# Attention in turns of a whole pair of heads, with the clusters placed by ScalarE

## The chip, the cores and the metric

The kernel runs on one core of a Trainium2 chip. The metric is the device time of one execution in microseconds; for each kernel several executions are timed and their median is given. A profile of one execution shows what every engine did. The engines are TensorE (PE in the profile; its weight loads are PEld), VectorE (DVE), ScalarE (ACT), GpSimd (POOL) and SyncE (SP, which only issues transfers). Each has a queue of its own and they meet by semaphores.

## The reference

Two stages. The first is attention in which a query sees only the keys of its own cluster; the second sends each token to one of eight experts.

```python
B, H, S, D, C = 4, 8, 768, 64, 16
q_assign = argmax(q_n @ c_n.T)               # nearest of 16 centroids, all normalised
k_assign = argmax(k_n @ c_n.T)
mask   = q_assign[..., :, None] == k_assign[..., None, :]
scores = where(mask, scale * q @ k.T, -1e9)
attn   = softmax(scores);   attn_out = attn @ v
x = attn_out as rows (3072 tokens, 512)
expert_idx = argmax(x @ w_gate);  gate_w = softmax(x @ w_gate)[expert_idx]
y[rows of e] = relu(x[rows of e] @ w1[e]) @ w2[e]      # 8 experts, 512 -> 1024 -> 512
out = gate_w[:, None] * y
```

Inputs are random and in float32.

## The kernel before

The attention works on pairs of heads, `g` from 0 to 15 (4 batches, 4 pairs each); one head of a pair lies on partitions 0 to 63, the other on 64 to 127. A pair has 12 scores (two halves of the queries, six tiles of 128 keys). The mask is part of the score: the clusters of queries and keys, written as one-hots into `ohT` (the keys' scaled so that other clusters get a huge negative number), are multiplied and added to q times k in the same bank of PSUM. The engines' instructions stand in the order in which the program names them (a manual schedule), and each engine keeps to its order.

```python
def score(u):                                  # one of 12 of a pair
    ps = ps_s.tile([P, 2, 512], F32, name="sps")          # one of 3 buffers of two banks
    for a in range(2): matmul(ps[:, a, 0:HS], lhsT=qk[g][r, 1, ks],  rhs=qk[g][r, 0, qs], start=True,  stop=False)
    for a in range(2): matmul(ps[:, a, 0:HS], lhsT=ohT[g][r, 1, ks], rhs=ohT[g][r, 0, qs], start=False, stop=True)
    A[u] = ap.tile([P, 2, HS], F32, name="A")
    nc.scalar.activation(A[u], ps[:, :, 0:HS], AF.Exp, scale=D**-0.5)
    if j == 1: T = A[u-1] + 1e-9/P + A[u]                 # VectorE
    elif j > 1: T = T + A[u]                              # VectorE

def attend(u):                                 # O (64 rows of each head) += v.T @ A[u]
    for a in range(2): matmul(O[g, half][a*D:(a+1)*D, 0:HS], lhsT=rows[g, "v"][:, a, j, :], rhs=A[u][:, a, :], ...)

def finish(g, half): nc.scalar.copy(XT[g][:, half...], O[g, half])
def turn_blocks(g):  # VectorE turns q and k of a pair, two instructions
def similar(g):      # 4 matmuls with the centroids into a score buffer; VectorE turns the result (sim)
def assign(g):       # VectorE: maximum, is_ge; GpSimd: times first_c
def assign2(g):      # VectorE: maximum, is_equal, and the turn of the one-hots (ohs)
def put_k(g):        # VectorE: scale (kv, two instructions), then four transfers kv -> ohT
def put_q(g):        # ScalarE: four copies ohs -> ohT
def weigh(g):        # 12 matmuls: row sums (T) and gate logits (XT) into the bank mps; VectorE turns it (ls)
def keep(g, c0, c1): # VectorE turns XT (xb); four stores from GpSimd to x_rows
...
# the routing of the first three batches, worked out while the last batch is attended:
choose, count, slots1, one_hots1(0), one_hots1(1), tokens1, spread1   # VectorE, TensorE, some GpSimd
gather1(0), gather1(1)                                                # GpSimd: indirect loads of x_rows
turn_rows1                                                            # VectorE: xu, the rows turned
first_half(0, ...)                                                    # first layer of expert 0
```

PSUM before: three score buffers of two banks (`ps_s`), one bank for the products (`ps_o`), one for everything small (`ps_m`, the tile `mps`). The loop takes turns of six (`NB = 6`), with jobs put between them by `at(turn, part, job)`:

```python
for n in range(-4, NTURN + 5):
    for x in range(n * NB, (n + 1) * NB):
        score(x)                      # (jobs of part 2 after the fifth)
    jobs of part 0                    # weigh, turn_blocks, similar, put_q, ...
    for x in range(n * NB, (n + 1) * NB):
        attend(x)
    jobs of part 1                    # finish, assign2, put_k, keep, ...
```

Of the kernel before, what the change touches and what calls it, by code (L numbers as in the profile page):

```python
# [20 lines left out]
NB = 6  # L21
# [164 lines left out]
def kernel(  # L186
# [14 lines left out]
    P = 128  # L201
# [65 lines left out]
    ps_o = late.enter_context(tc.tile_pool(name="ps_o", bufs=1, space=PSUM))  # L267
    ps_m = late.enter_context(tc.tile_pool(name="ps_m", bufs=1, space=PSUM))
# [12 lines left out]
    def blocks_of(g):  # L281
        return sum(g["n"]) // 32

# [355 lines left out]
    def count(part):  # L639
        ps = ps_m.tile([P, 512], F32, name="mps")  # L640
        last = part["pr"][:, :, part["n"] - 1]
        nc.tensor.matmul(ps[:, 0:E], lhsT=lt_strict, rhs=last, start=True, stop=True)
        nc.tensor.matmul(ps[:, E : 2 * E], lhsT=ones_sq, rhs=last, start=True, stop=True)
        nc.vector.tensor_copy(part["cnt"].rearrange("p a e -> p (a e)"), ps[:, 0 : 2 * E])
# [67 lines left out]
    def spread(pool, parts, w, gi):  # L712

        ps = ps_m.tile([P, 512], F32, name="mps")
        for i in range(4):
            nc.tensor.matmul(
                ps[:, i * 2 * w : (i + 1) * 2 * w],
                lhsT=k_["spread"][:, i, :], rhs=parts, start=True, stop=True,
            )
        v = ps[:, 0 : 8 * w].rearrange("p (i h w) -> p h w i", h=2, w=w)  # L720
        tv, ta = numbers(pool, v[:, 0], v[:, 1], [P, w, 4])
        nc.vector.tensor_scalar(tv, ta, scalar1=4.0, scalar2=k_["quarter"], op0=ALU.mult, op1=ALU.add)
        nc.vector.tensor_copy(gi, tv)
# [5 lines left out]

    msched = ExitStack()  # L730
    msched.enter_context(tc.manual_schedule())
    with ExitStack() as actx:
# [4 lines left out]
        ap = actx.enter_context(tc.tile_pool(name="ap", bufs=NB + 1))  # L737
# [3 lines left out]
        xtp = actx.enter_context(tc.tile_pool(name="xtp", bufs=2))  # L741
# [34 lines left out]
        def load_v(g):  # L776
            b, hp = divmod(g, HP)
            t = rows[g, "v"] = ld.tile([P, 2, NQ, D], F32, name="v_in", bufs=3)
            nc.sync.dma_start(
                out=t.rearrange("p a j d -> p a (j d)"),  # L780
                in_=v[b, 2 * hp : 2 * hp + 2].rearrange("a (p j) d -> p a (j d)", j=NQ),
            )
# [13 lines left out]
        def idle_of(n):  # L796
            idle(ps_m.tile([P, 512], F32, name="mps"), n)

        ps = ps_m.tile([P, 512], F32, name="mps")
# [57 lines left out]
        def blocks():  # L857
            cps = ps_m.tile([P, 512], F32, name="mps")
            nc.tensor.transpose(cps[:, 0:P], cn.rearrange("p a d -> p (a d)"), ident)
            cview = cps[:, 0:P].rearrange("p (g a c) -> p g a c", a=2, c=C)  # L860
            for a in range(2):
                nc.vector.tensor_copy(cblk[a * D : (a + 1) * D, :, a, :], cview[a * D : (a + 1) * D, :, a, :])
# [79 lines left out]
        def put_q(g):  # L942

            t = sims.pop(g)
            for half in range(2):
                for a in range(2):
                    i, r, cols = places(half, a)
                    nc.scalar.copy(ohT[g][r, 0, cols], t[i])

        def put_k(g):  # L950

            t, kv = sims[g], asg.tile([P, 2, HS], BF16, name="kv")
            ohT[g] = ohTs[g % 2]
            for a in range(2):
                nc.vector.tensor_scalar(
                    kv[D:P, a, :], t[D:P], scalar1=big[D:P, a, 0:1], scalar2=big[D:P, a, 1:2], op0=ALU.mult, op1=ALU.add
                )
            for half in range(2):
                for a in range(2):
                    i, r, cols = places(half + 2, a)  # L960
                    nc.sync.dma_start(out=ohT[g][r, 1, (half * HS) : (half + 1) * HS], in_=kv[i, a, :])
# [22 lines left out]
        def score(u):  # L984
# [12 lines left out]
            if j == 1:  # L997
                T[g, half] = tp_.tile([P, 2, HS], F32, name="T", bufs=3)
                nc.vector.scalar_tensor_tensor(  # L999
                    T[g, half], in0=A[u - 1], scalar=1e-9 / P, in1=A[u], op0=ALU.add, op1=ALU.add  # L1000
                )
            elif j > 1:
                nc.vector.tensor_tensor(T[g, half], T[g, half], A[u], op=ALU.add)  # L1003
# [18 lines left out]
        rds, pads = {}, {}  # L1022

        def weigh(g):
# [4 lines left out]
            ps = ps_m.tile([P, 512], F32, name="mps")  # L1029
# [26 lines left out]
        def keep(g, c0, c1):  # L1056

            b, hp = divmod(g, HP)
            xb = xtp.tile([P, S], F32, name="xb")
            nc.vector.transpose(xb[:, 0 : c1 - c0], XT[g][:, c0:c1])  # L1060
            for quad in range(4):
                nc.gpsimd.dma_start(  # L1062
                    out=x_d[b * S + c0 : b * S + c1, quad, hp * 32 : (hp + 1) * 32].rearrange("(n t) d -> t n d", t=32),
                    in_=xb[quad * 32 : (quad + 1) * 32, 0 : c1 - c0].rearrange("p (n d) -> p n d", d=32),
                )
# [44 lines left out]
        TG = UG // NB  # L1110
        TH = NQ // NB
        NTURN = NG * TG
        at(0, 1, place_consts)
        at(6, 1, place_consts2)
        for g in range(NG):
            n = g * TG
            if g == 0:
                at(-4, 0, turn, g, 0)
                at(-4, 0, load_next)
                at(-4, 0, blocks)  # L1120
                at(-4, 1, turn, g, 1)
                at(-3, 0, similar, g)
                at(-3, 0, assign, g)
                at(-3, 0, assign2, g)
                at(-3, 0, put, g)
            elif g == 1:
                at(-2, 1, idle_of, 20)
                at(0, 0, turn_blocks, g)
                for f in (similar, assign, assign2, put_k):
                    at(0, 1, f, g)  # L1130
                at(1, 0, put_q, g)
            else:
                at(n - 3, 0, turn_blocks, g)
                at(n - 2, 0, similar, g)
                at(n - 2, 0, assign, g)
                at(n - 2, 1, assign2, g)
                at(n - 2, 1, put_k, g)
                at(n - 1, 0, put_q, g)
            at(n, 1, finish, g, 0)
            at(n + 1, 1, finish, g, 1)  # L1140
            if g < NG - 1:
                at(n + 2, 0, weigh, g)
                at(n + 2, 1, keep, g, 0, S)
                if g % HP == HP - 1:
                    at(n + 3, 0, gate, g // HP)
                    at(n + 4, 0, gate2, g // HP)
# [18 lines left out]
        def tokens1():  # L1165
            ps = ps_m.tile([P, 512], F32, name="mps")[:, 0 : 2 * NP]
            tokens(ps, oh_r1, oh_c1, NF)
            rc1[1] = indices(pl, ps, NP, s_idx1)
# [21 lines left out]

        n = (NG - HP) * TG
        at(n + 1, 1, choose, pl, front)
        at(n + 2, 1, count, front)
        at(n + 2, 1, slots1)
        at(n + 3, 0, one_hots1, 0)
        at(n + 3, 1, one_hots1, 1)
        at(n + 5, 2, tokens1)
        at(n + 5, 1, spread1)
        at(n + 5, 1, gather1, 0)
        at(n + 6, 1, gather1, 1)  # L1200
        at(n + 7, 0, turn_rows1, 0)

        n = NG * TG
        at(n - 1, 0, keep, NG - 1, 0, HS)
        at(n, 0, weigh, NG - 1)
        at(n, 0, keep, NG - 1, HS, S)
        at(n, 0, first_half, 0, 0, FB // 4)
        at(n, 0, gate, B - 1)
        at(n, 0, gate2, B - 1)
        at(n, 0, keep_pads, B - 1)  # L1210
        at(n, 0, turn_rows1, 1)
        at(n, 1, first_half, 0, FB // 4, FB // 2)
        at(n + 1, 0, first_half, 0, FB // 2, FB)
        for g in range(2, NG):
            at(max(g * TG - 6, -1), 1, load_qk, g)
            at(max(g * TG - 5, -1), 1, load_v, g)
        for b in range(B - 1):

            at((b + 1) * HP * TG + 2, 1, keep_pads, b)
# [14 lines left out]
        for e in range(2):  # L1234
            for i in range(DB):
                at(HP * TG * (e + 1) - 4 + 2 * i + 1, 0, early, e, i)

        for n in range(-4, NTURN + 5):
            for x in range(n * NB, (n + 1) * NB):
                if 0 <= x < NU:  # L1240
                    score(x)
                if x == n * NB + 4:
                    for f, a in jobs.get((n, 2), ()):
                        f(*a)
            for f, a in jobs.get((n, 0), ()):
                f(*a)
# [3 lines left out]
            for f, a in jobs.get((n, 1), ()):  # L1250
                f(*a)


    mctx = ExitStack()
# [4 lines left out]
    with tc.tile_pool(name="sm", bufs=1) as sm:  # L1259
# [34 lines left out]
        tok_ps = ps_m.tile([P, 512], F32, name="mps")[:, 0 : 2 * NC]  # L1294
# [19 lines left out]
        bps = ps_m.tile([P, 512], F32, name="mps")[:, 0:1]  # L1314
# [178 lines left out]
```

## Time and profile before

| | |
|---|---|
| time, median of 3 runs | 712.38 us (711.19 to 713.41) |
| span of the profiled execution | 716.9 us |
| TensorE busy | 686.9 us (96%) |
| VectorE busy | 484.6 us (68%) |
| ScalarE busy | 266.9 us (37%) |
| GpSimd busy | 251.1 us (35%) |
| attention, first score to last product | from 15.2 to 342.1 us |

A line of a group reads: line of the kernel, engine, operation, written tile <- read tiles, shape, count | busy us, mean ns of one | idle time of the engine just before them and what ended most of it. A line of a timeline reads: start in us, length in us, engine, line, operation and tiles, how many were merged into it, and in brackets how long the engine was idle before it and who ended that. A float32 matmul is recorded as two.

### The profile page before, as it was taken

Reading aid. Unit: us, or ns where it says so; the run is one execution under the profiler, and the core shown is the slowest. Engines: PE = TensorE matmul, PEld = TensorE weight load, DVE = VectorE, ACT = ScalarE, POOL = GpSimd, SP = SyncE. Lnnn points to the kernel's source line nnn. Section 1 sums busy time; section 2 is a strip of 40 time slices with the busy share of each in tenths; the row PEclk is TensorE's granted clock in tenths of the full one; section 3 lists DMA queues with packets and bytes.
Section 4 is the critical chain, followed back from the end, with each engine's and each line's share of the span. In section 5 each row is a group of like instructions: output and inputs, shape, how many; then the busy total and the mean of one; then the engine's idle time right before and its main releaser. Section 6 shows DMA issues by size and latency. Waiting matters only on the chain.

```text
span 716.9 us, 12015 instructions
## 1 busy us (share of the span) xinstructions
PE 686.9 (96%) x4603; PEld 443.2 (62%) x4603; DVE 484.6 (68%) x769; ACT 266.9 (37%) x410; POOL 251.1 (35%) x327
## 2 busy tenths in 40 slices
PE   8999999999999899989998779999999999999994
PEld 7444444444444444535645649879888787987761
DVE  5898888878988789997586146866576667655300
ACT  3665556655665467645111012121311112131100
POOL 4022121222222112346735652645255373313101
PEclk9999999999999999999999999999999999999998
DMA  8345697777767555211535245767686666758540
GB/s 148 65 88 93 129 151 139 144 120 135 127 134 128 96 94 94 32 29 36 62 125 166 61 167 194 263 232 270 208 302 205 233 219 248 267 185 308 188 134 20
DMA packets 152420, 108.20 MB, mean 151 GB/s; under 512 B 116513, under 2 KB 122529, under 8 KB 152354
## 3 DMA queue, kind: packets, MB, share of 16 engines
q1 hardware_dynamic: 138146, 78.89, 41.1%
q0 software_dynamic: 8640, 19.63, 12.4%
q10 hardware_dynamic: 5568, 8.83, 4.2%
q8 instruction: 38, 0.62, 0.4%
q14 instruction: 28, 0.23, 0.1%
HBM read 93.06 MB, written 13.30 MB: 148 GB/s over the span
## 4 chain that ended last, share of the span: by engine, by line
PE 52%; issue 16%; DVE 12%; POOL 7%; SPq 4%; DMA 3%; another core or an unknown queue 3%; ACT 1%; ACTq 0%; DVEq 0%; POOLq 0%
PE sps L991 11%; PE O L1011 9%; PE sps L495 8%; PE sps L318 6%; PE sps L383 6%; PE sps L517 5%; DVE T L1003 4%; POOL xg L289 3%; PE sps L994 3%; DMA ohT<-kv 2%; POOL out_dram L338 2%; SPq L1097 2%; PE sps L354 1%; PE mps L1033 1%
## 5 line engine op out<-in xcount | busy, mean ns | idle before, releaser
L289 POOL DMA_INDIRECT xg<-x_rows,g_idx x104 | 116.6, 1121 | 133.1 <-DVE xgT L305 92.4
L996 ACT ACTIVATE A<-sps 128x768 f32<-128x768 f32 x192 | 151.6, 813 | 25.6 <-PE sps L994 23.5
L991 PE MATMUL sps<-qk 64*128 64x384 f32 x768 | 159.6, 493 | 1.6 <-DVE sim L911 1.5
L1003 DVE TENSOR_TENSOR T<-T,A 128x768 f32<-128x768 f32 x128 | 122.7, 958 | 14.3 <-ACT A L996 0.8
L1011 PE MATMUL O<-A,v_in 128*64 128x384 f32 x768 | 130.9, 490 | 0.0
L991 PEld LDWEIGHTS sps<-qk 64*128 64x128 f32 x768 | 66.8, 186 | 54.5 <-issue 48.2
L1011 PEld LDWEIGHTS O<-A,v_in 128*64 128x64 f32 x768 | 52.3, 137 | 74.4 <-issue 71.7
L1045 POOL COPY dens<-ls 128x12 f32<-128x12 f32 x16 | 3.3, 204 | 207.1 <-DVE ls L1041 207.1
L383 PE MATMUL sps<-w,h_sb 128*128 128x512 f32 x144 | 65.1, 605 | 3.0 <-DVE h_sb L326 3.0
L994 PE MATMUL sps<-ohT 64*128 64x384 bf16 x384 | 64.7, 323 | 2.8 <-DMA ohT<-kv 2.7
L338 POOL DMA_INDIRECT out_dram<-zo,s_idx x32 | 38.6, 1207 | 72.0 <-ACT zo L334 28.6
L318 PEld LDWEIGHTS sps<-xgT,w 128*128 128x128 f32 x448 | 51.0, 192 | 3.7 <-issue 3.7
L1019 ACT COPY xT<-O 128x384 f32<-128x384 f32 x32 | 15.3, 479 | 101.2 <-PE O L1011 86.5
L318 PE MATMUL sps<-xgT,w 128*128 128x128 f32 x448 | 51.3, 275 | 0.0
L1062 POOL DMA_DIRECT2D x_rows<-xb x68 | 48.7, 724 | 4.3 <-DVE xb L1060 2.3
L383 PEld LDWEIGHTS sps<-w,h_sb 128*128 128x128 f32 x144 | 27.4, 195 | 35.0 <-issue 31.2
L999 DVE SCALAR_TENSOR_TENSOR T<-A 128x768 f32<-128x768 f32 x32 | 30.6, 958 | 25.2 <-ACT A L996 24.8
L495 PE MATMUL sps<-xs,w1s 128*128 128x144 f32 x288 | 41.3, 297 | 3.1 <-issue 3.0
L495 PEld LDWEIGHTS sps<-xs,w1s 128*128 128x128 f32 x288 | 37.8, 195 | 9.7 <-issue 5.0
L994 PEld LDWEIGHTS <-ohT 64*128 64x128 bf16 x384 | 20.3, 94 | 28.7 <-DMA ohT<-kv 4.8
L361 ACT COPY zc<-sps 32x512 f32<-32x512 f32 x24 | 13.9, 579 | 60.8 <-PE sps L354 49.6
L328 ACT ACTIVATE h_sb<-sps 128x512 f32<-128x512 f32 (+1 forms) x18 | 9.6, 578 | 69.6 <-PE sps L318 51.0
(256 smaller groups left out, 924.1 us busy)
## 6 DMA issues: line engine op xcount, KB each, us to landing
w<-in_moe_w_dram SPq DMA_DIRECT2D x28, 2048.0 KB, 9.1
w<-in_moe_w_dram ACTq DMA_DIRECT2D x16, 512.0 KB, 6.0
v_in<-in_v_dram SPq DMA_DIRECT2D x16, 384.0 KB, 4.5
q_in<-in_q_dram SPq DMA_DIRECT2D x60, 96.0 KB, 3.5
k_in<-in_k_dram SPq DMA_DIRECT2D x60, 96.0 KB, 3.9
x_rows<-xb POOLq DMA_DIRECT2D x60, 96.0 KB
xg<-x_rows,g_idx POOLq DMA_INDIRECT x104
ohT<-kv SPq DMA_DIRECT2D x60, 24.0 KB, 4.4
```

The lines of the kernel that those rows point to most:

```text
L289: nc.gpsimd.indirect_dma_start(out=g["xg"][:, n, :], out_offset=None, in_=x_q[0 : 4 * g["rows"], :], in_offset=bass.IndirectOffsetOnAxis(a ...
L318: nc.tensor.matmul(o, lhsT=g["w"][0][:, c, fb * P : (fb + 1) * P], rhs=g["xT"][:, c, :cols], start=(c == 0), stop=(c == DB - 1),)
L338: ins = nc.gpsimd.indirect_dma_start(out=out[:, :], out_offset=bass.IndirectOffsetOnAxis(ap=g["si"](j)[0:m], axis=0), in_=zo[0:m], in_offs ...
L383: nc.tensor.matmul(zp, lhsT=g["h"][:, fb, j * P : (j + 1) * P], rhs=g["w"][1][:, fb, :], start=(fb == 0), stop=(fb == FB - 1),)
L495: nc.tensor.matmul(o, lhsT=a[:, c, f * P : (f + 1) * P], rhs=b[:, c, :], start=(c == 0), stop=(c == KH - 1),)
L517: nc.tensor.matmul(ps[:, 0, 0:DH], lhsT=a[:, f, :], rhs=b[:, f, :], start=(f == 0), stop=(f == FH - 1),)
L991: nc.tensor.matmul(ps[:, a, 0:HS], lhsT=qk[g][r, 1, ks], rhs=qk[g][r, 0, qs], start=True, stop=False)
L994: nc.tensor.matmul(ps[:, a, 0:HS], lhsT=ohT[g][r, 1, ks], rhs=ohT[g][r, 0, qs], start=False, stop=True)
L996: nc.scalar.activation(A[u], ps[:, :, 0:HS], AF.Exp, scale=D**-0.5)
L1003: nc.vector.tensor_tensor(T[g, half], T[g, half], A[u], op=ALU.add)
L1011: nc.tensor.matmul(O[g, half][a * D : (a + 1) * D, 0:HS], lhsT=rows[g, "v"][:, a, j, :], rhs=a_[:, a, :], start=(j == 0), stop=(j == NQ - 1),)
L1062: nc.gpsimd.dma_start(out=x_d[b * S + c0 : b * S + c1, quad, hp * 32 : (hp + 1) * 32].rearrange("(n t) d -> t n d", t=32), in_=xb[quad * 3 ...
```

## The change

A turn becomes a whole pair: 12 scores, then 12 products. With that the array changes its tiling between scores and products once a pair instead of twice. The clusters of the next pair are placed by ScalarE alone, eight small instructions while the products run, in place of VectorE's scaling and four transfers; so no score waits for a transfer. The small bank `ps_m` is given up for a second bank of products, and the small products take a score buffer instead (`bank()`). The jobs move to the new turns.

```diff
-NB = 6
+NB = 12
...
-    ps_o = late.enter_context(tc.tile_pool(name="ps_o", bufs=1, space=PSUM))
-    ps_m = late.enter_context(tc.tile_pool(name="ps_m", bufs=1, space=PSUM))
+    ps_o = late.enter_context(tc.tile_pool(name="ps_o", bufs=2, space=PSUM))
...
+    def bank():
+        return wide()[:, 0, :] if "attention" in pools else ps_o.tile([P, 512], F32, name="O")
...   (count, spread, weigh, tokens, idle_of: ps_m.tile(...) becomes bank())
-        ap = actx.enter_context(tc.tile_pool(name="ap", bufs=NB + 1))
+        ap = actx.enter_context(tc.tile_pool(name="ap", bufs=NB))
...   (v_in: 3 buffers become 2; T: 3 become 4; xT and xb: 2 become 1, both halves of the last xb in one)
-        def put_q(g):
+        def put_by_scalar(g):
             t = sims.pop(g)
+            ohT[g] = ohTs[g % 2]
             for half in range(2):
                 for a in range(2):
                     i, r, cols = places(half, a)
+                    k = slice(D + half * 32, D + half * 32 + 32)
                     nc.scalar.copy(ohT[g][r, 0, cols], t[i])
+                    nc.scalar.activation(
+                        ohT[g][r, 1, cols], t[k], AF.Identity, scale=big[k, a, 0:1], bias=big[k, a, 1:2]
+                    )
-        def put_k(g):
-            t, kv = sims[g], asg.tile([P, 2, HS], BF16, name="kv")
-            ohT[g] = ohTs[g % 2]
-            for a in range(2):
-                nc.vector.tensor_scalar(
-                    kv[D:P, a, :], t[D:P], scalar1=big[D:P, a, 0:1], scalar2=big[D:P, a, 1:2], op0=ALU.mult, op1=ALU.add
-                )
-            for half in range(2):
-                for a in range(2):
-                    i, r, cols = places(half + 2, a)
-                    nc.sync.dma_start(out=ohT[g][r, 1, (half * HS) : (half + 1) * HS], in_=kv[i, a, :])
...
+        at(-1, end, turn_blocks, 1)
+        for f in (similar, assign, assign2):
+            at(0, 4, f, 1)                      # after the fifth score of pair 0
         for g in range(NG):
+            at(g, end, finish, g, 0)
+            at(g, end, finish, g, 1)
+            if g + 2 < NG:
+                at(g, mid, turn_blocks, g + 2)
+                at(g, end, similar, g + 2)
+                at(g, end, assign, g + 2)
+            if g < NG - 1:
+                at(g, end, keep, g, 0, S)
+                at(g + 1, mid, weigh, g)
+                at(g, mid, put_by_scalar, g + 1)
+            if g + 2 < NG:
+                at(g, end, assign2, g + 2)
+            if g % HP == HP - 1 and g < NG - 1:
+                at(g + 1, mid, gate, g // HP)
+                at(g + 1, end, gate2, g // HP)
+                at(g + 1, end, keep_pads, g // HP)
...
+        n = NG - HP                             # pair 12
+        at(n, end, choose, pl, front)
+        at(n + 1, mid, count, front)
+        at(n + 1, mid, slots1)
+        at(n + 1, mid, one_hots1, 0)
+        at(n + 1, end, one_hots1, 1)
+        at(n + 2, 4, tokens1)                   # after the fifth score of pair 14
+        at(n + 2, 8, spread1)                   # after the ninth
+        at(n + 2, 8, gather1, 0)
+        at(n + 3, mid, gather1, 1)
+        at(n + 3, mid, turn_rows1, 0)
...
+            for i, x in enumerate(range(n * NB, (n + 1) * NB)):
+                score(x)
+                run(n, i)
+            run(n, mid)                         # between scores and products
+            for x in range(n * NB, (n + 1) * NB):
+                attend(x)
+            run(n, end)
```

## The prediction

> **What bounds the kernel now.** I read the page first (shares of the engines, costliest groups), then the timelines of TensorE, VectorE and ScalarE over a few pairs of heads, then TensorE's waits, and last the order of instructions that the changed kernel gives each engine. From the page, the busy line and three groups, and from the fuller list of groups the copies that place the clusters of the queries (busy us, mean ns | idle before):
>
> ```profile
> PE 686.9 (96%) x4603; PEld 443.2 (62%) x4603; DVE 484.6 (68%) x769; ACT 266.9 (37%) x410; POOL 251.1 (35%) x327
> ...
> L996 ACT ACTIVATE A<-sps 128x768 f32<-128x768 f32 x192 | 151.6, 813 | 25.6 <-PE sps L994 23.5
> L991 PE MATMUL sps<-qk 64*128 64x384 f32 x768 | 159.6, 493 | 1.6 <-DVE sim L911 1.5
> L1003 DVE TENSOR_TENSOR T<-T,A 128x768 f32<-128x768 f32 x128 | 122.7, 958 | 14.3 <-ACT A L996 0.8
> ```
>
> ```profile
> L948 ACT COPY ohT<-ohs 32x384 bf16<-32x384 bf16 x60 | 30.5, 509 | 1.2
> ```
>
> Attention fills 15 to 342 us; TensorE is its bound. One pair of heads in the timeline of TensorE (start, length):
>
> ```profile
> 46.26 0.92 PE L991 MATMUL sps<-qk 64*128 64x384 f32 x4
> ...
> 47.17 0.81 PE L991 MATMUL sps<-qk 64*128 64x384 f32 x4
> ...
> 47.98 0.81 PE L991 MATMUL sps<-qk 64*128 64x384 f32 x4
> ...
> 51.30 4.09 PE L1011 MATMUL O<-A,v_in 128*64 128x384 f32 x24
> 55.32 0.92 PE L991 MATMUL sps<-qk 64*128 64x384 f32 x4
> ...
> 60.37 0.86 PE L1033 MATMUL mps<-T,one_row 128*32 128x192 f32 x16
> 61.04 0.51 PE L1033 MATMUL mps<-xT,wg 128*32 128x192 f32 x8
> 61.37 0.83 PE L904 MATMUL sps<-qk,cblk 128*32 128x384 f32 x8
> 62.12 4.09 PE L1011 MATMUL O<-A,v_in 128*64 128x384 f32 x24
> 66.15 0.92 PE L991 MATMUL sps<-qk 64*128 64x384 f32 x4
> ```
>
> From 46.26 to 66.15 is 19.89 us without an idle stretch: 5.04 (six scores), 4.02 (six products), 5.05, 1.75 (weigh and similar), 4.03. Scores follow each other by 0.81. Where TensorE waited, it was for these:
>
> ```profile
> 239.41 0.51 PE L994 MATMUL sps<-ohT 64*128 64x384 bf16 x2 [1.94 <-DMA ohT<-kv]
> ...
> 313.22 0.92 PE L991 MATMUL sps<-qk 64*128 64x384 f32 x4 [1.46 <-DVE sim L911]
> ...
> 322.64 0.24 PE L716 MATMUL mps<-hlb,to_quarters 128*128 128x8 bf16 x4 [1.16 <-DVE tv L697]
> ```
>
> The first is what the change removes. The other two stand where the routing of the first three batches is worked out between the scores: there VectorE is late.
>
> **What the Trainium skill says.** "TensorEngine Tiling (Array Packing)", Key Properties: a change of tiling mode, not of tile alone, drains the array. The trace agrees: six scores at 0.81 would be 4.85, the stretch is 5.04, so two changes cost 0.19, about 0.1 us each. "TensorE: Matmul & The Clock Gate", Architectural detail: ScalarE and VectorE take their instructions strictly in order, and matmuls keep theirs. The timelines agree, and all stalls below rest on it. The same page, "What's actually happening": an idle stretch of about 3.4 us brings the clock back to half. The stretches agree: after TensorE had been idle for most of 393 to 396 us the granted clock was 0.58 from 396 to 400, and 0.50 from 413 to 416 after another such gap. "ScalarE: Activation LUTs", Table sets: identity is in every table set. No instruction of the kernel before shows it; the order of ScalarE in the changed kernel has the same two table loads at the start and none after them, so I count none.
>
> **The change part by part.** All times are of one pair, from the start of its scores.
>
> 1. Fewer changes of form. Before, a pair has five (scores to products, back, scores to weigh, similar to products, back); after, four (scores to weigh, to products, to similar, to scores). One at 0.1 us in 15 pairs: −1.5 us. A pair becomes 19.8.
>
> 2. Clusters without a transfer. Removed are 60 transfers (4 a pair) and two VectorE operations of 0.4 us a pair. The starts of the products that follow similar lie 19.89 apart, except for 20.77, 21.23 and 22.17 where the clusters were late: 0.88 + 1.34 + 2.28 = 4.5 us that go. The new ScalarE work is 4 activations of 32x384 beside the 4 copies (2.10 us in the timeline); at the copies' 0.51 the eight take 4.1 us. They stand behind the twelve exponentials, which end some 1 us after the scores (9.9), so at 10.7, and end at 15; the products run until 18.9. ScalarE has then 9.8 + 4.1 + 1.0 = 14.9 of 19.8 us. It follows the twelve scores: six exponentials with a backlog took 4.41 us, 0.74 each against 0.81 for a score. Path: −4.5 us, nothing back.
>
> 3. VectorE over a whole pair. Order after: similar's transpose, assign, keep, assign2, ten additions, weigh's transpose, two turns of q and k. From its timeline (105.13 to 118): the first part 109.74 − 105.13 = 4.6; additions 5.13 for five, 10.3; weigh 0.55; turns 1.84: 17.3 us of 19.8. The result that TensorE needs next (qk for similar) is there at 17.4 and wanted at 18.9. So in a plain pair TensorE does not wait, with 1.5 us to spare. In pairs 4, 8 and 12 the gate comes right behind weigh and waits for GpSimd (1.25 us after the reciprocal) and adds 0.44 ahead of the turns: qk at 19.1, about 0.2 us of wait each, +0.6.
>
> 4. Banks. The bank of weigh, count, tokens and spread is now one of the three that the scores rotate through, and it stays taken until VectorE has read it. In a plain pair that is hidden: weigh's bank is read at 15.4, in the products. In pair 0 similar of pair 1 stands after the fifth score, and its bank is read only after four additions (18.57 + 4.1 = 22.7, then 0.5): TensorE, after two more scores, is there at 21.7. With the wait that was there before (0.22 and a slow similar) I count +1.0.
>
> 5. Pairs 13 and 14. VectorE has in pair 13 beside its 17.3: choose 1.8, count and slots 3.1, the first one-hots 1.5. That is 23.7 us against 20.3 on TensorE. So it reads similar's bank 4.1 us into pair 14; the third score needs that bank at 1.6: wait 2.5. The fifth score ends at 6.5. Tokens wants the second one-hots, on VectorE at 9.6, and then GpSimd's share (two of about 0.8 us, behind four stores of 0.72): 11.0, wait 4.5. Its bank is read after four additions, 14.2: the eighth score waits 0.9. Spread's bank is read after three more additions: the last score waits 0.7. Together 8.6 us, and with the idle 4.5 us the clock falls, so tokens and the next scores run slower: some 1.3 more. Before, these pairs had 3.1 us of stall (the products' distance of 23.12 against 20.0 for the same matmuls). Net +6.8 us.
>
> 6. The end. Before, the first layer of the experts waited 0.89 us for xu. After, VectorE turns those rows while the last products run, so −0.9. VectorE also waited 3.16 us for the store of x_rows before the last gate, which one shared buffer avoids; but after it TensorE has 15.8 us of matmuls before count, so that is off the path. From there the order of the expert part is as before.
>
> Sum: −1.5 − 4.5 + 0.6 + 1.0 + 6.8 − 0.9 = +1.5 us on 712.4.
>
> **The rivals.** (a) The stall of step 5 does not come, or is half of it: then the other terms give −5 us, 706 or so. For it: the kernel before stalls only 3.1 us with the same work, and the places after the fifth and ninth score look chosen. Against it: VectorE has 23.7 us of work in pair 13, whatever the places. (b) VectorE becomes the bound of every pair: it has 1.5 us to spare, and if each addition took 0.2 us more, TensorE would wait half a microsecond in 13 pairs: +6 to +10, 720. For it: it is 17.3 of 19.8 already. Against it: it loses 0.8 us of work a pair, and no other engine gets any that it hands on. (c) ScalarE becomes the bound, should an activation with scale and bias from memory cost 1 us: 4 x 0.5 x 1 more, 17 us of 19.8, still hidden behind the products. It would take over 1.8 us each to show. (d) The gain is larger than I see because fewer stops keep the clock up. Against it: the granted clock was 1.00 from 20 to 341 us already.
>
> **Range and chances.** The sum says 713.9; (a) pulls down and (b) up, and I give (a) a little more because my walk adds every stall to the path: 712.5. All gains without any stall would be about 10 us, so 2% (698) is all but out of reach. A loss of 2% (726.6) needs (b) in full on top of step 5. Range 705 to 720.
>
> **What would show it.** Starts of the products 19.8 apart in plain pairs; no wait for a transfer of the clusters; TensorE's waits gathered in the pair with tokens, named VectorE's sim, oh_r or GpSimd's oh_c; additions of VectorE starting 4.7 us into a pair; placing done before the second half of the products ends. I am wrong if plain pairs differ from 19.8 by more than 0.1, if the pair of tokens loses under 4 or over 13 us, or if the expert part moves by more than 3 us.

## The result, and the profile after

The changed kernel takes 699.63 us (median of four executions, 699.1 to 700.08), the kernel before, run beside it, 711.79 (709.65 to 713.41). The ratio is 0.9831, with a 95% interval of 0.9802 to 0.9859: 12 us less, where 712.5 us, hardly a change, was predicted. The profiled execution has a span of 698.3 us.

The page of the changed kernel, busy line and the groups that answer to those shown of before (busy us, mean ns | idle before):

```profile
PE 676.6 (97%) x4603; PEld 439.3 (63%) x4603; DVE 471.8 (68%) x739; ACT 310.8 (45%) x470; POOL 250.1 (36%) x327
...
L992 ACT ACTIVATE A<-sps 128x768 f32<-128x768 f32 x192 | 153.5, 812 | 32.4 <-PE sps L990 28.6
L987 PE MATMUL sps<-qk 64*128 64x384 f32 x768 | 159.9, 495 | 2.7 <-DVE sim L915 2.2
...
L999 DVE TENSOR_TENSOR T<-T,A 128x768 f32<-128x768 f32 x128 | 122.7, 959 | 13.0
...
L990 PE MATMUL sps<-ohT 64*128 64x384 bf16 x384 | 64.0, 326 | 0.0
...
L955 ACT ACTIVATE ohT<-ohs,big 32x384 bf16<-32x384 bf16 x60 | 42.0, 700 | 0.8
```

The work is the same and takes as long: 768 score matmuls of 495 ns, 128 additions of 959 ns. What is gone is idle time before the score's second half, the product of the clusters (L990): 0.0. New is ScalarE's row L955, the keys' clusters, 0.70 us each. One pair in the timeline of TensorE (start, length):

```profile
46.26 7.96 PE L1007 MATMUL O<-A,v_in 128*64 128x384 f32 x48
54.15 0.85 PE L908 MATMUL sps<-qk,cblk 128*32 128x384 f32 x8
54.93 0.92 PE L987 MATMUL sps<-qk 64*128 64x384 f32 x4
...
64.82 0.86 PE L1029 MATMUL sps<-T,one_row 128*32 128x192 f32 x16
...
65.94 7.96 PE L1007 MATMUL O<-A,v_in 128*64 128x384 f32 x48
```

From products to products it is 65.94 − 46.26 = 19.68 us. Twelve products take 54.15 − 46.26 = 7.89, where before twice six took 4.02 + 4.03 = 8.05. The stalls are gathered in one place, the pair in which the first three batches are routed. TensorE there (in brackets: how long it was idle, and for whom):

```profile
296.06 0.92 PE L987 MATMUL sps<-qk 64*128 64x384 f32 x4 [2.16 <-DVE sim L915]
...
302.48 0.38 PE L691 MATMUL sps<-oh_c,oh_r 128*128 128x8 bf16 x9 [3.42 <-POOL oh_c L681]
302.79 1.65 PE L987 MATMUL sps<-qk 64*128 64x384 f32 x4
...
304.55 1.49 PE L987 MATMUL sps<-qk 64*128 64x384 f32 x4
...
311.36 0.92 PE L987 MATMUL sps<-qk 64*128 64x384 f32 x4 [0.41 <-DVE tv L700]
```

and VectorE's timeline in the same stretch:

```profile
294.15 1.35 DVE L684 TENSOR_TENSOR oh_r<-iota_f,rc 128x1152 bf16<-128x1152 f32 x1
295.42 0.58 DVE L915 STREAM_TRANSPOSE sim<-sps 128x384 f32<-128x384 f32 x1
...
300.05 1.35 DVE L684 TENSOR_TENSOR oh_r<-iota_f,rc 128x1152 bf16<-128x1152 f32 x1
301.31 1.01 DVE L995 SCALAR_TENSOR_TENSOR T<-A 128x768 f32<-128x768 f32 x1
```

VectorE empties the bank of similar only at 296.0, behind the first one-hots; the third score needs that bank and waits. Then TensorE stands before tokens until the second one-hots are there. After the longer stop four scores take 1.76, 1.60, 1.60 and 1.13 us from start to start instead of 0.81; the granted clock was 0.50 from 302.4 to 308. The products are 30.14 us apart here (283.34 to 313.48). By what they hold it would be 19.68 and, by my estimate from the lengths of these matmuls, 0.9 for tokens and spread, 20.6: the stalls cost 9.6.

Set against the first profile of before, this does not explain the gain. The attention, first score to last product, was 326.9 us there and is 325.3 here, 1.6 less. From the first layer of the experts to the end of the span it was 372.8 and is 356.9, 15.9 less, in a part where the change touches almost nothing. That asked for a second profile of the kernel before.

### The profile page after: what moved, and what is told of

It reads as the page before. It is cut to its first block, busy times and chain, and to the rows that moved or that the text cites. A ratio compares the mean times of both kernels' runs of the same rounds, so it can differ in the third digit from the quotient of the medians.

```text
span 698.3 us, 11976 instructions
## 1 busy us (share of the span) xinstructions
PE 676.6 (97%) x4603; PEld 439.3 (63%) x4603; DVE 471.8 (68%) x739; ACT 310.8 (45%) x470; POOL 250.1 (36%) x327
## 4 chain that ended last, share of the span: by engine, by line
PE 70%; issue 15%; POOL 6%; DVE 5%; DMA 1%; ACT 0%; ACTq 0%; POOLq 0%; DVEq 0%
PE sps L987 17%; PE O L1007 16%; PE sps L321 9%; PE sps L498 8%; PE sps L386 6%; PE sps L520 5%; PE sps L990 4%; POOL xg L292 3%; POOL out_dram L341 2%; PE sps L1029 2%; DVE T L999 2%; PE sps L908 2%; PE sps L357 1%; DMA xg<-x_rows,g_idx 1%; PE sps L798 1%
## 5 line engine op out<-in xcount | busy, mean ns | idle before, releaser
L992 ACT ACTIVATE A<-sps 128x768 f32<-128x768 f32 x192 | 153.5, 812 | 32.4 <-PE sps L990 28.6
L1007 PE MATMUL O<-A,v_in 128*64 128x384 f32 x768 | 127.4, 488 | 0.0
L1007 PEld LDWEIGHTS O<-A,v_in 128*64 128x64 f32 x768 | 53.7, 137 | 67.7 <-issue 65.9
L990 PE MATMUL sps<-ohT 64*128 64x384 bf16 x384 | 64.0, 326 | 0.0
L386 PE MATMUL sps<-w,h_sb 128*128 128x512 f32 x144 | 63.1, 592 | 0.0
L926 POOL TENSOR_TENSOR sim<-sim,first_c 128x384 f32<-128x384 f32 x14 | 14.0, 1003 | 87.8 <-DVE sim L925 87.8
L955 ACT ACTIVATE ohT<-ohs,big 32x384 bf16<-32x384 bf16 x60 | 42.0, 700 | 0.8
L498 PEld LDWEIGHTS sps<-xs,w1s 128*128 128x128 f32 x288 | 36.0, 190 | 5.0 <-DVE xs L409 4.2
L337 ACT COPY zo<-sps 128x512 f32<-128x512 f32 x12 | 7.0, 586 | 71.0 <-PE sps L386 65.2
L498 PE MATMUL sps<-xs,w1s 128*128 128x144 f32 x288 | 37.9, 288 | 0.0
```

Source lines behind the costliest of these rows:

```text
L386: nc.tensor.matmul(zp, lhsT=g["h"][:, fb, j * P : (j + 1) * P], rhs=g["w"][1][:, fb, :], start=(fb == 0), stop=(fb == FB - 1),)
L498: nc.tensor.matmul(o, lhsT=a[:, c, f * P : (f + 1) * P], rhs=b[:, c, :], start=(c == 0), stop=(c == KH - 1),)
L955: nc.scalar.activation(ohT[g][r, 1, cols], t[k], AF.Identity, scale=big[k, a, 0:1], bias=big[k, a, 1:2])
L990: nc.tensor.matmul(ps[:, a, 0:HS], lhsT=ohT[g][r, 1, ks], rhs=ohT[g][r, 0, qs], start=False, stop=True)
L1007: nc.tensor.matmul(O[g, half][a * D : (a + 1) * D, 0:HS], lhsT=rows[g, "v"][:, a, j, :], rhs=a_[:, a, :], start=(j == 0), stop=(j == NQ - 1),)
```

## The experiments

None of these kernels leaves out part of the computation. Times and ratios first, then each with its reason. The kernel before, run beside them, took 713.96 us (first four kernels) and 715.02 (last three).

| kernel | us, median (range) | ratio to before | 95% interval |
|---|---|---|---|
| before, once more | 713.95 (711.31 to 715.36) | 0.9996 | 0.9971 to 1.0021 |
| turns of six, ScalarE places all clusters | 708.65 (706.09 to 712.26) | 0.9933 | 0.9909 to 0.9957 |
| turns of a pair, transfers kept | 705.94 (705.37 to 707.64) | 0.9907 | 0.9877 to 0.9937 |
| changed kernel, tokens later | 694.21 (692.66 to 694.35) | 0.9732 | 0.9694 to 0.9770 |
| turns of six, VectorE places the keys' clusters | 703.06 (701.57 to 703.44) | 0.9820 | 0.9791 to 0.9848 |
| turns of a pair, VectorE places the keys' clusters | 704.77 (704.69 to 705.13) | 0.9850 | 0.9824 to 0.9876 |
| changed kernel, tokens and first one-hots later | 691.40 (691.34 to 691.48) | 0.9662 | 0.9637 to 0.9687 |

**The kernel before, once more.** No edit; a second execution with its profile.

> The kernel before once more, for a second profile of it. In the first profile the first expert layer starts at 344.1 us before and 341.4 after (2.7 us apart), but the ends are 716.9 and 698.3 (18.6 apart): the larger share lies behind the attention. Theory A (that share is a property of the program before: the stops of TensorE near 410 and 424 to 431 us come from how its work stands): this profile shows stops at the same places, and from the start of the first layer to the end it takes again 368 us or more. Theory B (they are an accident of that one execution): it takes about 357 to 360 as after does, and then most of the gain must stand in the attention, which this profile would show ending later than 342.

The span is 711.1 us. From the page, the clusters' matmuls, and from its list of transfers the clusters' (the last number is the median from issue to landing, in us); first in the profile that the prediction used, then in this one:

```profile
L994 PE MATMUL sps<-ohT 64*128 64x384 bf16 x384 | 64.7, 323 | 2.8 <-DMA ohT<-kv 2.7
...
ohT<-kv SPq DMA_DIRECT2D x60, 24.0 KB, 4.4
```

```profile
L994 PE MATMUL sps<-ohT 64*128 64x384 bf16 x384 | 68.5, 327 | 7.8 <-DMA ohT<-kv 7.8
...
ohT<-kv SPq DMA_DIRECT2D x60, 24.0 KB, 5.8
```

TensorE, four of the seven waits:

```profile
97.44 0.33 PE L994 MATMUL sps<-ohT 64*128 64x384 bf16 x1 [0.78 <-DMA ohT<-kv]
98.77 0.50 PE L994 MATMUL sps<-ohT 64*128 64x384 bf16 x1 [1.00 <-DMA ohT<-kv]
...
163.80 0.68 PE L994 MATMUL sps<-ohT 64*128 64x384 bf16 x2 [2.86 <-DMA ohT<-kv]
...
249.02 0.55 PE L994 MATMUL sps<-ohT 64*128 64x384 bf16 x2 [1.98 <-DMA ohT<-kv]
```

and SyncE's queue ahead of the first three of them:

```profile
91.50 3.00 SPq L961 DMA_DIRECT2D ohT<-kv  x4
...
145.83 8.54 SPq L1097 DMA_DIRECT2D x_rows<-pad  x16
154.46 0.62 SPq L779 DMA_DIRECT2D v_in<-in_v_dram  x1
155.18 3.67 SPq L961 DMA_DIRECT2D ohT<-kv  x4
```

The first profile had 2.8 us of idle time before these matmuls and a landing of 4.4 us. This one has 7.8 and 5.8. Behind two of the stops slow scores come on top: from 98.8 and from 164.1 us, two scores each took 1.4 to 1.8 us at a granted clock of 0.50, 3.1 us more than at 0.81. The part of weigh that reads xT should come every 19.89 us; over its first twelve distances it came 14.5 us late in all (23.76 for the third, 24.51 for the sixth). The idle time and the slow scores make 10.9 of them; the rest is not taken apart here. The first profile, counted in the same way, has 4.5. So the term that the change removes is three times what I took. The attention (first score to last product) took 337.1 us here and 326.9 in the first profile; from the first layer of the experts to the end of the span it is 357.2 here and was 372.8 there. That is theory B. The first execution was fast where the change works and slow where it doesn't.

These lines show why the margin is thin. Ahead of 163.80, kv is finished in VectorE's timeline at 154.5 us. The queue is busy with 16 small stores and a load until 155.1 and then issues the four transfers one by one until 158.9; the score wants its clusters at 160.9 (163.80 less the wait), and the first of them lands at 163.75, 8.6 us after its issue. The queue holds the first one up by 1.3 us here (its half of kv was there at 153.9), less than half of the wait. Ahead of 249.02 it holds longer: kv was finished at 240.5 and the first transfer went out at 243.15. The other five waits, 3.0 of the 7.8 us, came with the queue free: the transfers of 91.50 went out while kv was being written and still took 5.9 and 6.6 us. So the stores on the queue are one part and slow landing the other; no run here moves the stores alone. Landing takes 1.7 us at the least in this profile and 8.6 at the most. The Trainium skill ("DMA: Bandwidth & Descriptors", Issuing engines are not separate DMA queues) says that transfers of all issuing engines run on the same 16 DMA engines and interleave. The spread of the landing fits that, but no run here varies the other traffic alone.

**Turns of six, ScalarE places all clusters.** One part of the change alone.

```diff
 (kernel before)
-        def put_q(g): ...   def put_k(g): ...      # copies; scale and four transfers
+        def put_by_scalar(g): ...                  # eight instructions of ScalarE, as in the change
...
-                at(n - 2, 1, put_k, g)
-                at(n - 1, 0, put_q, g)
+                at(n - 1, 0, put_by_scalar, g)
```

> The kernel before with one part of the change: turns of six as they were, but ScalarE places the clusters of the keys too, and the four transfers and VectorE's two scalings a pair are gone. Theory 1 (the waits for these transfers are what the attention gains): the products are 19.9 us apart in every pair without routing, 4.5 us fewer in the attention, about 707 us. Theory 2 (the transfers also stood in the way of others behind the attention): more than 8 us, near 702. Theory 3 (turns of a whole pair are the gain): 711 to 712, since ScalarE's 4 more activations of 0.70 us in a product phase of 4 us delay the next exponentials.

It gains 5 us, between theories 1 and 3 and not all of the transfers' wait. TensorE, six products and the scores of a pair's second half:

```profile
72.94 4.09 PE L1003 MATMUL O<-A,v_in 128*64 128x384 f32 x24
76.96 0.92 PE L983 MATMUL sps<-qk 64*128 64x384 f32 x4
...
80.11 0.92 PE L983 MATMUL sps<-qk 64*128 64x384 f32 x4 [0.45 <-ACT A L988]
```

and ScalarE beside it:

```profile
73.89 0.51 ACT L950 COPY ohT<-ohs 32x384 bf16<-32x384 bf16 x1
...
78.14 0.70 ACT L951 ACTIVATE ohT<-ohs,big 32x384 bf16<-32x384 bf16 x1
78.86 0.48 ACT L1011 COPY xT<-O 128x384 f32<-128x384 f32 x1
79.24 4.41 ACT L988 ACTIVATE A<-sps 128x768 f32<-128x768 f32 x6
```

The eight placements take 4.95 us (73.89 to 78.84), and six products only 4.02 (72.94 to 76.96). So the next exponential starts at 79.24, 2.3 us after its score did; the three score buffers fill up and the fourth score waits. It happens fourteen times, and a plain pair is 20.62 us instead of 19.89. Wait for transfers is exchanged for wait for ScalarE. With twelve products, 7.89 us, the same eight are hidden. Placing by ScalarE and the turn of a pair belong together.

**Turns of a pair, transfers kept.** The other part alone.

```diff
 (changed kernel)
-        def put_by_scalar(g): ...
+        def put_q(g): ...   def put_k(g): ...      # as before
-                at(g, mid, put_by_scalar, g + 1)
+                at(g, mid, put_q, g + 1)
 ...
                 at(g, end, assign2, g + 2)
+                at(g, end, put_k, g + 2)
```

> The changed kernel with the transfers back: turns of a pair, but the keys' clusters go through VectorE's scaling and four transfers again, issued a whole pair ahead of their use (small helper tiles with one buffer in place of two, so that it fits). Theory 1 (transfers): with so much time ahead no wait comes, so 700 to 702; if SyncE's queue is held by the stores of the gates even so, waits of 1 to 2 us in pairs 5, 9 and 13 and 703 to 705. Theory 3 (turns): 700 to 702 and the products 19.7 apart.

What TensorE waited for in the attention (line, releaser: us, times, longest):

```profile
PE sps L691 <- POOL oh_c L681: 2.7, 1, 2.7
PE sps L995 <- DVE sim L915: 2.4, 1, 2.4
PE sps L908 <- DVE qk L894: 1.0, 3, 0.4
...
```

705.94 us, above both ranges. There is no wait for a transfer, though landing was about as slow as in the second profile of before (median 5.5 us, at most 7.8): here they are issued a pair ahead. So the waits of before are a question of margin, not of the transfers as such. Plain pairs are 19.68 us, and yet the kernel is slower than the changed one by ratio (0.9907 against 0.9831, intervals apart): VectorE has the two scalings more in every pair, waits for qk appear in the gate pairs (20.8 to 20.9 us), and the routing pair is 32.86 instead of 30.69.

**Turns of six, VectorE places the keys' clusters.** Only the transfers go: VectorE writes straight into ohT, in four instructions instead of two.

```diff
 (kernel before, put_k)
-            kv[D:P, a, :] = t[D:P] * big[...] + big[...]          # two, then four transfers kv -> ohT
+            for half in range(2):
+                for a in range(2):                                # four, no transfer
+                    nc.vector.tensor_scalar(ohT[g][r, 1, cols], t[k], scalar1=big[k, a, 0:1], scalar2=big[k, a, 1:2], ...)
```

> The kernel before with its transfers alone taken away: turns of six, queries' clusters by ScalarE as before, the keys' clusters written by VectorE straight into ohT (four instructions of 0.4 us a pair in place of two and four transfers). Theory 1 (the waits for the transfers, 14.5 us in the second profile of before and 4.5 in the first, are what the change mostly removed): pairs without routing 19.9 apart, the attention some 14 us shorter, time 699 to 702 and runs that differ by less than 3 us. Rival (the first profile's 4.5 us is the usual amount): 707 to 709. Rival (VectorE, 0.8 us more a pair, is late for similar): pairs of 20.2 and more, 704 to 707.

703.06 against 715.02 us: 12.0 less, 1 us above theory 1's range. TensorE, from the products of one pair to those of the next, and its waits in the attention and the first layer:

```profile
61.72 4.09 PE L1010 MATMUL O<-A,v_in 128*64 128x384 f32 x24
...
81.61 4.09 PE L1010 MATMUL O<-A,v_in 128*64 128x384 f32 x24
```

```profile
PE sps L990 <- DVE sim L911: 2.7, 1, 2.7
PE mps L716 <- DVE tv L697: 2.0, 1, 2.0
PE sps L318 <- DVE xu L305: 1.5, 1, 1.5
PE sps L990 <- ACT A L995: 1.3, 1, 1.3
...
```

Its pairs without routing are 19.89 us, but for one of 21.47 with the wait for ScalarE. Here nothing but the path of the keys' clusters has changed, so this measures the transfers' wait by itself, less what new waits cost: 1.6 us in that pair, and 2.9 in the two pairs with the routing (20.51 and 26.75 us by weigh, against 20.43 and 23.93 in the second profile of before). It also says that the whole change is not shown to bring more than this one part: the ratios are 0.9831 and 0.9820, with intervals that overlap for the most part. The spans of one execution each, 698.3 and 701.3, are 3.0 apart.

**Turns of a pair, VectorE places the keys' clusters.** The changed kernel with VectorE in ScalarE's place for the keys.

```diff
 (changed kernel, put_by_scalar)
-                    nc.scalar.activation(ohT[g][r, 1, cols], t[k], AF.Identity, scale=big[k, a, 0:1], bias=big[k, a, 1:2])
+                    nc.vector.tensor_scalar(ohT[g][r, 1, cols], t[k], scalar1=big[k, a, 0:1], scalar2=big[k, a, 1:2], ...)
```

> The changed kernel with the keys' clusters placed by VectorE in place of ScalarE, again without transfers, turns of a pair. VectorE gets 1.6 us more a pair: 18.9 of 19.7. If it is as near to the bound as the prediction had it (17.3 of 19.7 and 1.5 us to spare), plain pairs stay at 19.7, the pairs with a gate grow by about 1.5 us each and pair 14 by 1.6 to 3: 705 to 708, as with the transfers back. If ScalarE's part in the change is only to be free of transfers: 699 to 701.

TensorE's waits in the attention:

```profile
PE sps L987 <- DVE sim L915: 5.4, 4, 4.0
PE sps L987 <- DVE tv L700: 1.8, 2, 1.2
PE sps L691 <- POOL oh_c L681: 0.9, 1, 0.9
...
```

Four instructions of 0.37 us are 1.5 us of VectorE a pair. Plain pairs stay at 19.68, so these still fit; the gate pairs are 20.57 to 21.4, and the routing pair 32.33. So the work costs where VectorE has no room: 704.77 us is just under the 705 to 708 expected for that case, and the span of 703.0 us is 4.7 longer than that of the changed kernel. By ratio the two (0.9850 and 0.9831) have intervals that overlap, so that the ratios alone leave the size of it open.

**The changed kernel, tokens later.** The second term of my sum, the stalls of the routing pair, tried by itself: tokens moves from behind the fifth score of its pair to the end of the scores, spread and the first gather behind its products.

```diff
 (changed kernel)
-        at(n + 2, 4, tokens1)
-        at(n + 2, 8, spread1)
-        at(n + 2, 8, gather1, 0)
+        at(n + 2, mid, tokens1)
+        jobs[n + 2, end][:0] = [(spread1, ()), (gather1, (0,))]
```

> The changed kernel with three jobs moved: the tokens' matmuls stand behind the twelve scores of pair 14 in place of behind the fifth, spread and the first gathers behind its products. Theory: the stop of pair 14 (its products start 30.1 us after those of pair 13, a plain pair takes 19.7) comes from the tokens' wait for the one-hots and from the score buffers that tokens and spread hold; then the distance falls to about 22.5, the rows are gathered some 4 us later, which costs the first layer at most 2 us, and the time is 693 to 695. Rival: the gather is on the path, the first layer waits for what the scores save, and the time stays at 699 to 700.

694.21 us. What is left of the stalls in the timeline of TensorE:

```profile
296.02 0.92 PE L987 MATMUL sps<-qk 64*128 64x384 f32 x4 [2.15 <-DVE sim L915]
...
296.93 1.47 PE L987 MATMUL sps<-qk 64*128 64x384 f32 x4
...
298.50 1.50 PE L987 MATMUL sps<-qk 64*128 64x384 f32 x4
```

The waits for oh_c and tv are gone. The pair is 24.33 us instead of 30.69 by weigh; tokens then costs in the next, 19.62 instead of 18.89. The first layer starts at 335.72 instead of 341.38, without a wait of TensorE: the rows are ready just in time.

**The changed kernel, tokens and the first one-hots later.** On top of that, the first one-hots move behind VectorE's turn of similar.

```diff
 (kernel of the experiment above)
-        at(n + 1, mid, one_hots1, 0)
+        at(n + 1, end, one_hots1, 0)
```

> The kernel with the tokens later, and the first one-hots moved behind the assign of pair 15 too, so that VectorE reads similar's bank 1.5 us sooner. Theory: the third score's wait of 2.15 us falls to 0.6, the clock does not fall to half for the two scores behind it (1.3 us), and VectorE, whose work is the same, still has the indices ready for spread: 2.5 to 3 us less, about 691.5. Rival: VectorE sets the end of pair 14 and the wait moves to spread: 693.5 to 694.5.

TensorE in that pair:

```profile
294.36 0.92 PE L987 MATMUL sps<-qk 64*128 64x384 f32 x4 [0.65 <-DVE sim L915]
...
303.31 0.51 PE L1029 MATMUL sps<-xT,wg 128*32 128x192 f32 x8
303.75 0.60 PE L691 MATMUL sps<-oh_c,oh_r 128*128 128x8 bf16 x18
```

The wait for similar falls from 2.15 to 0.65 us, and no score after it is slow. 691.40 us is the best of all kernels here: 8.2 below the changed kernel's 699.63 by the medians, 8.7 by the profiled spans, and by ratio (0.9662) 3.4% below the kernel before. The products of the routing pair are 21.14 us apart instead of 30.14. Together with the experiment above it shows what the stalls of the routing pair cost, nearly all of the 9.6 us.

## Why the prediction was wrong

Predicted was 712.5 us, measured is 699.63, below the range. The sum, term by term, of the second profile of before (711.1 us) against the profile of after (698.3):

| step | predicted | measured | how |
|---|---|---|---|
| 1 changes of form | −1.5 | −3.4 | 19.89 − 19.68 = 0.21 a pair, 16 pairs |
| 2 transfers | −4.5 | −14.5 | lateness over twelve distances |
| 3 gate pairs | +0.6 | +0.4 | 19.82 − 19.68 in three pairs |
| 4 banks, pair 0 | +1.0 | −0.7 | below |
| 5 routing pair | +6.8 | +6.3 | 9.6 of stalls; before 3.3 (products 23.29 apart, against 20.0) |
| 6 first layer | −0.9 | −0.8 | 1.80 to 1.04 us after the last product |
| sum | +1.5 | −12.7 | the spans say −12.8 |

**Step 2 failed, in its size.** "0.88 + 1.34 + 2.28 = 4.5 us that go" was read rightly from the profile I had, and the mechanism was right: no score waits for clusters now. But it was the wait of one execution. A second has 14.5, and the kernel that loses the transfers and nothing else is 12.0 us faster by its times. These 10 us are most of the 14 by which the sum is off. Why the same transfers landed later in the second execution stays open. The first profile held the warning, and I passed over it: landing had a median of 4.4 us and a maximum of 5.5, for clusters wanted 5 to 7 us after kv. Where landing and margin are about equal, the wait isn't a number that one execution gives. The times held another: its span of 716.9 us lay above all three times (711.19 to 713.41), so it was not a usual execution. It was 10 us short in the attention and 15 long behind it, so that against this one profile a sum over the attention alone is off by 4 us (+2.4 predicted without step 6, −1.6 found).

**Step 1** had the right cause and half the size. I took the cost of a change from the scores alone (5.04 against 4.85). The products have theirs too. Twelve scores take 9.89 (54.93 to 64.82) where twice six took 10.09, twelve products 7.89 where twice six took 8.05, and weigh and similar, now apart, 1.90 where together they took 1.75: 0.20 + 0.16 − 0.15 = 0.21. In plain pairs 19.68 stands in every kernel with turns of a pair, whoever places the clusters.

**Step 2's other half**, ScalarE: an activation takes 0.70 us and not the 0.51 of a copy; with the four copies that is 4.96 us (46.09 to 51.05 in the changed kernel's timeline). It lies in the products of 7.89, as step 2 said, and rival (c) does not come. The trace has the same two table loads at the start as before and none after them. Turns of six showed the other side: in 4.02 us it doesn't fit, and that kernel gains 5 us only.

**Step 3** held. VectorE has room in plain pairs (19.68, no wait), and a gate pair costs 0.14 us. The turn of a pair with transfers and the one with VectorE's placing put 0.8 and 1.5 us more on it, and the waits came in the gate and routing pairs first.

**Step 4** had the wrong sign. The eighth score of pair 0 starts 0.26 us late (22.34 instead of 22.08), right behind an exponential that ends at 22.29. The wait of about 1 us for similar's bank did not come: VectorE has read it at 23.09, and the ninth score follows at 23.25 without an idle stretch. And the slow similar and its wait in the kernel before, 1.61 − 0.83 + 0.22 = 1.0 us, are gone: 0.26 − 1.0 = −0.7.

**Step 5** held, in its places too: 2.16 us for sim where 2.5 was worked out, 3.42 for oh_c where 4.5, 0.41 for tv where 0.9 and 0.7; but the four slow scores cost 2.8 us and not 1.3 (6.09 against four times 0.81). Moving the jobs gave it back, 5 and then 8 us. Rival (a), that the stall does not come, falls; so does (b), that VectorE bounds every pair.

**Step 6** held. Rival (d), a gain from the clock, had a part in it that I missed: 3.1 of the 14.5 us are scores at half clock behind two of the waits, in a stretch where the first profile had shown a granted clock of 1.00 throughout.

Of the signs that I had named for being wrong, two came: plain pairs of 19.68, 0.12 from 19.8, and, set against the first profile, an expert part 15.9 us shorter (0.3 against the second).

The limit that I set, "all gains without any stall would be about 10 us", stood on step 2 and fell with it. Without most of the stalls the gain is 24 us, as the last experiment shows.

## What to carry to other kernels

Where a wait hangs on a transfer that lands about when it is wanted, compare the margin with the spread of the landing times and look at a second execution, before its cost in one profile goes into a sum. A longer turn gives small work a phase to hide in, but gathers the stalls of rare jobs: when the turn changes, place those jobs anew, by what the engine that feeds them has to do before them. And try the removal alone: here four VectorE instructions in place of the transfers brought about as much, by the ratios, as the whole change, until the rare jobs were moved.

## What the runs showed of the hardware

The landing of small transfers within SBUF, the same 60 of 24 KB in the same program, had a median of 4.4 us in one execution and 5.8 in another. The first trace shows the landing of only 15 of them and the second of 46; on the 15 that both show, the second is 0.8 to 1.9 us later in 14 and equal in one. The times do not decide whether the spread of the kernel before comes from this: it ran over 710.5 to 717.8 us in 22 executions and turns of six with VectorE's placing over 701.6 to 703.4 in four, but turns of six with ScalarE's placing, which has none of these transfers either, over 706.1 to 712.3 in ten. Why landing is slower in one execution isn't settled.

A stop of 2.15 us before the third score was followed by scores of 1.47 and 1.50 us in one kernel (tokens later), with a granted clock of 0.50 from 297 to 300, while in the changed kernel the same stop, 2.16 us at the same place, was followed by scores of 0.81 and a granted clock of 1.00. The Trainium skill ("TensorE: Matmul & The Clock Gate", What's actually happening) calls the window in which activity is judged about 3.4 us long and free-running, and gives half clock after at least one idle window. That it runs free could be why equal stops differ; no run here shows it. By the length of the window a stop of 2.15 us should not have been enough. Here it was, so a stop shorter than the window isn't safe.

Behind the attention the first profile of before was 15 us longer than every other run: 372.8 us from the first layer to the end of the span, and 356.9 to 357.2 in all the others. Its TensorE stood still several times between 410 and 431 us. It didn't come again, and what it was stays open.
